# Attention, routed experts and a feed-forward block in one kernel: rows stored in token order, experts' rows found from summed lists

## The chip, the cores and the metric

The kernel runs on one core of one Trainium2 chip. The metric is the device time of one execution in microseconds (us). The kernel before took 825.89 us, the median of three runs (821.13 to 826.58).

## What is computed

Inputs are 4 batches of 8 heads, 768 positions and head size 48, so 3072 tokens of 384 numbers.

```python
# 1. attention with a decaying state, for each batch and head, t = 0..767
cur   = outer(u * k[t], v[t])
y[t]  = r[t] @ (state + cur)
state = w[:, None] * state + outer(k[t], v[t])
# 2. x = y as 3072 rows of 384; each row goes to one of 8 experts
logits     = (x / |x|) @ (emb / |emb|).T / tau
expert_idx = argmax(logits);  gate = softmax(logits)[expert_idx]
out[mask]  = gate * (relu(x[mask] @ w1[e]) @ w2[e])      # 384 -> 1024 -> 384
# 3. a dense block over all rows, 384 -> 2048 -> 384
h = out @ w_in;  result = (h * clip(h + 3, 0, 6) / 6) @ w_out
```

## The kernel before

**Attention.** Positions are cut into 6 chunks of 128 (`c`), heads into 4 pairs (`hp`): 24 groups in order `i = 4c + hp`. Each group (all four batches at once) runs on TensorE the scores `a_ps` (L642), the diagonal part `m_ps` (L654), the outputs `y_ps` (L665, L669), the state's update `u_ps` (L676) and the transposes `x_ps` (L690) that put the result into token rows `x_t`. ScalarE copies the scores out (`a_m`, L645) and GpSimd masks them (L646); VectorE makes the scaled operands (`k_s` L625, `r_s` L626), `mv` and `y_sb`. Loads for a group are issued four groups ahead on SyncE (SP).

**Routing.** When the four groups of chunk `c` are done, `route(c)` runs as a generator, one step a group, during chunk `c + 1`: logits, argmax and the one-hot `ohot`, then ranks by matmuls with a triangle and with ones. Before, the rank places a token inside its chunk with the tokens sorted by expert, and four indirect transfers a chunk (L274, GpSimd's queue) scatter the rows of `x_t` (384 numbers, the gate, padding) into `xs_d` in DRAM.

**The first expert early.** After three chunks (`c == KC and hp == 3`, i = 15), `leader` takes the expert with most tokens so far. `shift` and `lead_rows` compute from the chunks' counts where its rows lie, `x_rows` (L373) gathers 256 of them, and `x_cols` scales them by the gate (L384, ScalarE), transposes them on TensorE (L391) and splits them into a high and a low part `xh`, `xl` (L392, L393). When the attention ends, `expert(0, ...)` runs over these 256 columns, with the last chunk's routing, `late_rows` (where the leader's other rows lie), `order` (experts by size) and `all_rows` between its steps. Then a second pass with the same weights takes the next 256 rows of the leader, gathered only then (`late`, L870), and experts 1 to 7 follow with fixed widths of 444 down to 378 columns; the gather and the transposes for an expert run under the expert before it.

**An expert** is eight steps `f`: `l1(f + 2)` (nine matmuls into one bank), `l2(f)` (nine into three accumulators `acc`), then `between(f)`. Each product is three matmuls of float32r operands (high by high, low by high, high by low: L398 to L400), so a pass is 144 matmuls, each behind its own weight load of 128 columns.

**Order.** Within an engine, instructions keep the order that a planner gave them, which lays the program out by estimated times; matmuls marked `pin` keep program order, and `behind(x, n)` keeps `x` behind the instruction recorded under `n`. At run time each engine and each DMA queue takes its list strictly in order, so an instruction that waits holds up all behind it.

Of the kernel before, what the change touches and what calls it, by code (L numbers as in the profile page):

```python
# [8 lines left out]
F32 = mybir.dt.float32  # L9
# [25 lines left out]
NE = 256  # L35
NB = 512

CAPS = [NE, 444, 420, 408, 400, 392, 388, 378]
# [6 lines left out]
def rwkv_moe_kernel(ctx, tc, dT, tokA, wuT, uw, emb, tau, w1, w2, win, wout, out):  # L45
# [13 lines left out]
    y_d = dram.tile([NT, DM], F32, name="y_d")  # L59
    wf_d = [dram.tile([128, WCH], F32, name=f"wf_d{j}") for j in range(4)] if wide else None  # L60

    actx = ExitStack()
# [20 lines left out]
    wrk = st_p.tile([128, E * RPT * E], F32, name="wrk")  # L83
    zrow = st_p.tile([128, E * NT // 128], I32, name="zrow")
    nc.gpsimd.memset(zrow, 0)
    nums = const.tile([128, 3], F32, name="nums")
    three, hlf, viol = (nums[:, i:i + 1] for i in range(3))
# [9 lines left out]
    delta = const.tile([128, NCH, E], F32, name="delta")  # L97
# [20 lines left out]
    lead_i = const.tile([128, 2], I32, name="lead_i")  # L118
    n0 = lead_f[:, 1:2]
# [59 lines left out]
    def prep_w(j, lo_eng, after=None, st=None, later=None):  # L179
# [6 lines left out]
        def piece(c0):  # L186
            sl = slice(c0, c0 + WCH // 3)
            cp = nc.scalar.copy(out=hi[:, sl], in_=st[:, sl])
            if after:
                behind(cp, after)  # L190
# [3 lines left out]
            if after == "x_t":  # L194
                behind(sub, "y_s")
        for c0 in range(0, WCH, WCH // 3):
# [14 lines left out]
    def route(c, x_t, sm, xT, st_p, group="rows", pin=lambda i: i):  # L211
# [31 lines left out]
        aft = sm.tile([128, B, E], BF16, name="aft", tag="aft")  # L243
        nc.vector.tensor_tensor(out=aft, in0=iot, in1=idx_b, op=ALU.is_gt)
# [5 lines left out]
        rc_ps = psM.tile([128, B + 2, E], F32, name="r_ps", tag="m")  # L250
        r_ps, c_ps = rc_ps[:, 0:B], rc_ps[:, B:]
# [5 lines left out]
        for i, t in enumerate((oh, aft)):  # L257
            for b in range(B):
                pin(nc.tensor.matmul(c_ps[:, i], lhsT=ones, rhs=t[:, b], start=(b == 0), stop=(b == B - 1), skip_group_check=True))
        at = sm.tile([128, B, E], F32, name="at", tag="at")  # L260
        nc.vector.tensor_tensor(out=at, in0=r_ps, in1=oh, op=ALU.mult)
# [116 lines left out]
    def x_cols(rows, n, pool, width=NB, after=None):  # L378
# [3 lines left out]
        for t in range(rt):  # L382
            pn = min(128, n - t * 128)
            mul = nc.scalar.mul(rows[0:pn, t, 0:DM], rows[0:pn, t, 0:DM], rows[0:pn, t, DM:DM + 1])  # L384
            if after:
                behind(mul, after)
# [828 lines left out]
```

## Time and profile before

| | us |
|---|---|
| median of 3 runs | 825.89 |
| lowest, highest | 821.13, 826.58 |
| the profiled execution, its span | 824.2, 822.4 |

| engine | busy us | share of the span |
|---|---|---|
| PE (TensorE) | 784.0 | 95% |
| DVE (VectorE) | 494.7 | 60% |
| ACT (ScalarE) | 331.7 | 40% |
| POOL (GpSimd) | 218.9 | 27% |

The profile is one execution. PE's shares are highest from 205 us to the end, in the experts and the dense block. PEld is the weight load, which lies beside a matmul. A matmul's record is longer than the distance to the next one, since they are pipelined: the distance of starts is what one costs in a stream. "[3.40 <-ACT a_m L645]" behind an instruction means that its engine sat idle for 3.40 us before it and which instruction ended that.

### The profile page before, as it was taken

Reading aid. Unit: us, or ns where it says so; the run is one execution under the profiler, and the core shown is the slowest. Engines: PE = TensorE matmul, PEld = TensorE weight load, DVE = VectorE, ACT = ScalarE, POOL = GpSimd, SP = SyncE. Lnnn points to the kernel's source line nnn. Section 1 sums busy time; section 2 is a strip of 40 time slices with the busy share of each in tenths; the row PEclk is TensorE's granted clock in tenths of the full one; section 3 lists DMA queues with packets and bytes.
Section 4 is the critical chain, followed back from the end, with each engine's and each line's share of the span. In section 5 each row is a group of like instructions: output and inputs, shape, how many; then the busy total and the mean of one; then the engine's idle time right before and its main releaser. Section 6 shows DMA issues by size and latency. Waiting matters only on the chain. (4 is left out here: it accounts for less than half of the span.)

```text
span 822.4 us, 13576 instructions
## 1 busy us (share of the span) xinstructions
PE 784.0 (95%) x5178; PEld 698.3 (85%) x5179; DVE 494.7 (60%) x1014; ACT 331.7 (40%) x644; POOL 218.9 (27%) x239
## 2 busy tenths in 40 slices
PE   6899879889999999999999999999999999999994
PEld 4678666679999999998989998899999999999984
DVE  8789866463868777859478788552343334333331
ACT  3434435425455445545444333432333333333331
POOL 5667666443242144212101111210011002001001
PEclk9999998999999999999999999999999999999998
DMA  9968693234655566452322222110000001001001
GB/s 257 277 216 237 203 290 123 79 97 149 224 186 177 199 197 216 147 181 83 113 68 70 57 58 59 39 38 1 1 10 29 1 1 39 1 1 39 0 1 38
DMA packets 30552, 86.42 MB, mean 105 GB/s; under 512 B 4620, under 2 KB 12865, under 8 KB 30480
## 3 DMA queue, kind: packets, MB, share of 16 engines
q1 hardware_dynamic: 25312, 70.81, 28.2%
q0 software_dynamic: 5168, 14.68, 5.0%
q8 instruction: 42, 0.69, 0.4%
q14 instruction: 30, 0.25, 0.1%
HBM read 72.84 MB, written 12.63 MB: 104 GB/s over the span
## 5 line engine op out<-in xcount | busy, mean ns | idle before, releaser
L399 PE MATMUL l<-xl,whi 128*128 128x512 f32 (+8 forms) x504 | 186.4, 370 | 0.0
L398 PE MATMUL l<-xh,whi 128*128 128x512 f32 (+8 forms) x504 | 184.4, 371 | 1.9 <-DVEq L1074 1.6
L400 PE MATMUL l<-xh,wlo 128*128 128x512 f32 (+8 forms) x504 | 185.4, 369 | 0.0
L434 DVE SCALAR_TENSOR_TENSOR rg<-rg,l 128x512 f32<-128x512 f32 x96 | 65.8, 687 | 132.0 <-ACT rg L433 131.8
L433 ACT ACTIVATE rg<-l,nums 128x512 f32<-128x512 f32 x96 | 65.7, 689 | 169.8 <-PE l L400 160.1
L449 PE MATMUL o<-wlo,hh 128*128 128x384 f32 x384 | 128.6, 335 | 0.4 <-POOL wlo L1102 0.4
L448 PE MATMUL o<-whi,hh 128*128 128x384 f32 x384 | 128.0, 336 | 0.5 <-ACT hh L435 0.5
L450 PE MATMUL o<-whi,hl 128*128 128x384 f32 x384 | 123.9, 335 | 0.0
L398 PEld LDWEIGHTS l<-xh,whi 128*128 128x128 f32 x504 | 94.9, 189 | 13.4 <-issue 2.8
L400 PEld LDWEIGHTS l<-xh,wlo 128*128 128x128 f32 x504 | 95.1, 189 | 12.9
L399 PEld LDWEIGHTS l<-xl,whi 128*128 128x128 f32 x504 | 95.0, 189 | 10.2
L436 DVE TENSOR_TENSOR hl<-rg,hh 128x512 fp32r<-128x512 f32 x96 | 66.7, 697 | 43.5 <-ACT hh L435 42.9
L1132 POOL DMA_INDIRECT out_dram<-o_t,ctok x20 | 20.6, 1032 | 254.4 <-ACT o_t L1130 250.9
L435 ACT CAST hh<-rg 128x512 fp32r<-128x512 f32 x96 | 59.4, 621 | 68.4 <-DVE rg L434 52.5
L448 PEld LDWEIGHTS o<-whi,hh 128*128 128x128 f32 x384 | 72.0, 188 | 5.2 <-ACT hh L435 0.8
L449 PEld LDWEIGHTS o<-wlo,hh 128*128 128x128 f32 x384 | 72.1, 188 | 4.2 <-POOL wlo L1102 0.7
L399 PE MATMUL acc<-hl,whi 128*128 128x256 f32 (+7 forms) x216 | 71.8, 334 | 0.2 <-DVE hl L495 0.2
L450 PEld LDWEIGHTS o<-whi,hl 128*128 128x128 f32 x384 | 71.7, 188 | 0.3
L400 PE MATMUL acc<-hh,wlo 128*128 128x256 f32 (+7 forms) x216 | 72.0, 334 | 0.0
L495 DVE SCALAR_TENSOR_TENSOR hl<-l,hh 128x256 fp32r<-128x256 f32 (+7 forms) x72 | 38.1, 542 | 53.9 <-ACT hh L494 53.7
L494 ACT ACTIVATE hh<-l 128x256 fp32r<-128x256 f32 (+7 forms) x72 | 33.5, 481 | 91.6 <-PE l L400 88.7
L398 PE MATMUL acc<-hh,whi 128*128 128x256 f32 (+7 forms) x216 | 65.2, 335 | 0.7 <-DVE x L920 0.7
(215 smaller groups left out, 1176.0 us busy)
## 6 DMA issues: line engine op xcount, KB each, us to landing
wst<-in_w_dram SPq DMA_DIRECT2D x32, 768.0 KB, 4.3
rk_t<-in_dT_dram SPq DMA_DIRECT2D x24, 448.0 KB, 4.5
q<-in_win_dram SPq DMA_DIRECT2D x16, 384.0 KB, 3.3
q<-in_wout_dram SPq DMA_DIRECT2D x16, 384.0 KB, 3.3
vd<-in_dT_dram SPq DMA_DIRECT2D x24, 224.0 KB, 4.7
vt<-in_tok_dram SPq DMA_DIRECT2D x24, 224.0 KB, 4.5
tk<-in_tok_dram SPq DMA_DIRECT2D x24, 192.0 KB, 5.1
wf_d<-t SPq DMA_DIRECT2D x16, 192.0 KB, 4.1
```

The costliest lines, as they stand in the source:

```text
L398: pin(nc.tensor.matmul(ps, lhsT=w[0], rhs=x[0], start=first, stop=False))
L399: pin(nc.tensor.matmul(ps, lhsT=w[0], rhs=x[1], start=False, stop=False))
L400: pin(nc.tensor.matmul(ps, lhsT=w[1], rhs=x[0], start=False, stop=last))
L433: nc.scalar.activation(out=r6, in_=ps, func=AF.Relu, bias=three)
L434: nc.vector.scalar_tensor_tensor(out=gf, in0=r6, scalar=6.0, in1=ps, op0=ALU.min, op1=ALU.mult)
L435: nc.scalar.copy(out=gh, in_=gf)
L436: nc.vector.tensor_tensor(out=gl, in0=gf, in1=gh.bitcast(F32), op=ALU.subtract)
L448: pin(nc.tensor.matmul(acc[t], lhsT=gh[:, sl], rhs=wh[:, f % 4, :], start=(f == span[0]), stop=False))
L449: pin(nc.tensor.matmul(acc[t], lhsT=gh[:, sl], rhs=wl[:, f % 4, :], start=False, stop=False))
L450: pin(nc.tensor.matmul(acc[t], lhsT=gl[:, sl], rhs=wh[:, f % 4, :], start=False, stop=(f == span[1] - 1)))
L494: last["a"] = nc.scalar.activation(out=hh[:, 0:n], in_=ps[:, 0:n], func=AF.Relu).ins
L495: last["v"] = nc.vector.scalar_tensor_tensor(out=hl[:, 0:n], in0=ps[:, 0:n], scalar=0.0, in1=hh[:, 0:n].bitcast(F32), op0=ALU.max, op1=ALU ...
```

## The change

- Each chunk's rows go to `xs_d` in token order, one plain transfer a chunk on SP (`write`); the 24 scatters on GpSimd are gone.
- The rank now counts from the first chunk on (`cum` is added). VectorE makes two one-hots of each token, its row within a list's block of 128 (`at_row`) and its expert and block (`at_et`), and multiplies the second by the token's two digits (`who_et`). Four matmuls a chunk sum the digits at the token's place; `lists` adds the chunks up. A list entry is a row's number in `xs_d`. `shift`, `steps`, `late_rows`, `delta` and the matmuls over `aft` go.
- The early pass has 192 columns instead of 256, the late pass 256 as before, at a fixed place. The late rows are gathered during the early pass into a buffer of the attention (three transfers of 128 rows), and transposed before its last step.
- The early rows' scaling and transposes are spread over groups 18 to 21, each held behind that group's copies (`"x_t"`), and pinned on TensorE.
- The last chunk's third routing step moves behind `l1(2)`, and a fourth behind `l1(3)`; `order` and `all_rows` move two steps back, behind the list.
- The rare paths (`again`, `overflow`) and the places of conversion buffers follow; neither path runs here.

The core of the diff:

```diff
-NE = 256
+NE = 192
+NL = 256
...
-CAPS = [NE, 444, 420, 408, 400, 392, 388, 378]
+CAPS = [NE + NL, 444, 420, 408, 400, 392, 388, 378]
...
+    lp = ctx.enter_context(tc.tile_pool(name="lp", bufs=1))
...
+    nc.gpsimd.iota(row_i[:, 0:128], pattern=[[1, 128]], base=0, channel_multiplier=0)
...
+    nc.vector.tensor_copy(vals[:, :, 0], posn[:, 0:1].to_broadcast([128, NTILE]))
+    nc.vector.tensor_copy(vals[:, :, 1], row_i[:, 131:131 + NTILE])
...
-        for b in range(B):
-            pin(nc.tensor.matmul(r_ps, lhsT=ones, rhs=aft[:, b:b + 1, :].to_broadcast([128, B, E]), start=False, stop=False, skip_group_check=True))
...
-        dsti = sm.tile([128, B], I32, name="dsti", tag="dsti")
-        nc.vector.tensor_scalar(out=dsti, in0=rnk, scalar1=float(c * B * C), scalar2=None, op0=ALU.add)
...
-        nc.vector.tensor_tensor(out=delta[:, c], in0=c_ps[:, 1], in1=cum[:, c], op=ALU.subtract)
-
-        def scatter(b):
-            sc = nc.gpsimd.indirect_dma_start(out=xs_d[:, :], out_offset=bass.IndirectOffsetOnAxis(ap=dsti[:, b:b + 1], axis=0),
-                                              in_=x_t[:, b, :], in_offset=None, bounds_check=NT - 1, oob_is_err=False)
...
-        yield [lambda b=b: scatter(b) for b in range(B)]
+        if lists_too:
...
+            nc.vector.tensor_tensor(out=ge, in0=rnk.unsqueeze(2).to_broadcast([128, B, RPT - 1]), in1=row_f[:, 128:131].unsqueeze(1).to_broadcast([128, B, RPT - 1]), op=ALU.is_ge)
+            nc.vector.tensor_reduce(out=hi, in_=ge, axis=AX.X, op=ALU.add)
+            nc.vector.scalar_tensor_tensor(out=lo, in0=hi, scalar=-128.0, in1=rnk, op0=ALU.mult, op1=ALU.add)
+            nc.vector.scalar_tensor_tensor(out=et, in0=idx, scalar=float(RPT), in1=hi, op0=ALU.mult, op1=ALU.add)
...
+            nc.vector.tensor_tensor(out=at_row, in0=row_b.unsqueeze(1).to_broadcast([128, B, 128]), in1=lo.unsqueeze(2).to_broadcast([128, B, 128]), op=ALU.is_equal)
...
+            nc.vector.tensor_tensor(out=at_et, in0=row_b[:, 0:ET_].unsqueeze(1).to_broadcast([128, B, ET_]), in1=et.unsqueeze(2).to_broadcast([128, B, ET_]), op=ALU.is_equal)
...
+            nc.vector.tensor_tensor(out=who_et, in0=at_et.unsqueeze(2).to_broadcast([128, B, 2, ET_]), in1=vals[:, j0:j0 + B].unsqueeze(3).to_broadcast([128, B, 2, ET_]), op=ALU.mult)
+
+        def write():
+            loads["write"] = nc.sync.dma_start(out=xs_d.rearrange("(c b p) d -> c p b d", b=B, p=C)[c], in_=x_t).ins
+        yield [write]
+        l_ps = psM.tile([128, 2, ET_], F32, name="li_ps", tag="m")
+        for b in range(B):
+            pin(nc.tensor.matmul(l_ps, lhsT=at_row[:, b], rhs=who_et[:, b], start=(b == 0), stop=(b == B - 1)))
+        if c == 0:
+            nc.vector.tensor_copy(lists, l_ps)
+        else:
+            nc.vector.tensor_tensor(out=lists, in0=l_ps, in1=lists, op=ALU.add)
+        yield []
...
+    def lead_rows():
+
+        w = wrk[:, 0:2 * RPT * E].rearrange("p (v t e) -> p v t e", v=2, t=RPT)
+        sh = [128, 2, RPT, E]
+        nc.vector.tensor_tensor(out=w, in0=lists.rearrange("p v (e t) -> p v t e", e=E), in1=lead.unsqueeze(1).unsqueeze(1).to_broadcast(sh), op=ALU.mult)
...
         nc.vector.tensor_reduce(out=r, in_=w, axis=AX.X, op=ALU.add)
...
+        loads["list"] = nc.vector.scalar_tensor_tensor(out=ix0, in0=r[:, 1], scalar=128.0, in1=r[:, 0], op0=ALU.mult, op1=ALU.add).ins
...
+    LATE = [(t, 128) for t in range(NE // 128, RPT)]
...
+        parts = [scale] + [lambda k=k: third(k) for k in range(KD)]
...
+            mid(f)
             if f >= 0:
                 l2(f)
             between(f)
...
             if c == KC and hp == 3:
-                for f in rest:
-                    f()
-                rest = []
                 leader(cum[:, KC])
-
-                rows0 = x_rows(NE, e0p, ix0, KC * B * C)
+                rows0 = x_rows(in_rows(NE), e0p, ix0, tiles=2, known=KC * B * C)
...
-            if i == 20:
-                x0 = x_cols(rows0, NE, e0p, NE)
+            if i == 18:
+                x0 = x_cols(rows0, in_rows(NE), lp, NL, "x_t", cols, pin)
+            if cols and i >= 18:
+                cols.pop(0)()
...
+        def mid(f):
+            if f == 0:
+                for g in step(last_r, 1):
+                    g()
+            elif f == 1:
+                step(last_r, 1)
+                lead_rows()
+                late.append(x_rows(LATE, xp, ix0, "x", 2))
+                loads["late"] = loads["rows"]
 
         def between(f):
             if f == -2:
                 step(last_r, 1)
-            elif f == -1:
-                for g in step(last_r, 1):
+            elif f == 1:
+                chunks[3] = prep_w(3, nc.vector, "list", st3)
+            elif f == 2:
+                order("list")
+                all_rows()
+            elif f == NF1 - 2:
+                late.append(x_cols(late[0], LATE, lp, NL, later=cols, pin=pin, skip=NE % 128))
+                for g in cols[0:3]:
                     g()
-                late_rows()
-            elif f == 0:
-                order()
-                all_rows()
-            elif f == 1:
-                chunks[3] = prep_w(3, nc.vector, "relu", st3)
-        acc, _ = expert(0, x0, NE, between, pin)
+            elif f == NF1 - 1:
+                cols[3]()
+        late = []
+        acc, _ = expert(0, x0, NE, between, pin, mid)
...
-        late = x_rows(NE, mp, ix0[:, 2:4])
-        loads["late"] = loads["rows"]
...
-                dst = x2[d][:, bass.ds(at, n)]
+                dst = x2[d][:, bass.ds(at, n) if e else slice(NE, NE + NL)]
```

## Rows read from the trace of the kernel before

**Rows 1.** windows by chunk: busy us (instructions) PE, PEld, DVE, ACT, POOL; clock, DMA, GB/s

```profile
62.15:83.97 21.82, 21.82 (x312) 16.95 (x308) 20.15 (x45) 9.29 (x23) 17.45 (x19) 1.00 0.81 241
83.97:108.29 24.32, 22.20 (x312) 16.79 (x308) 21.67 (x64) 9.18 (x23) 17.10 (x19) 1.00 0.76 221
108.29:139.82 31.53, 27.30 (x313) 20.97 (x309) 19.11 (x46) 12.32 (x29) 19.98 (x23) 0.84 0.67 205
139.82:162.14 22.32, 18.79 (x219) 13.56 (x215) 11.88 (x35) 10.38 (x27) 10.80 (x11) 0.92 0.23 83
162.14:186.82 24.68, 19.62 (x172) 18.58 (x168) 13.44 (x62) 9.29 (x27) 8.79 (x10) 0.99 0.30 94
```

**Rows 2.** waits of PE over the span: us in total, times, longest

```profile
PE a_ps L642 <- ACT a_m L645: 3.4, 1, 3.4
PE tp L391 <- ACT rows L384: 3.4, 2, 2.6
...
PE tp L391 <- DVE xl L393: 1.8, 1, 1.8
...
PE r_ps L252 <- DVE ohot L242: 1.3, 1, 1.3
PE x_ps L690 <- DVE lead_f L312: 1.1, 1, 1.1
```

**Rows 3.** timelines of POOL and ACT around the early gather: start, us, instruction, wait before it

```profile
111.05 1.10 POOL L373 DMA_INDIRECT rows<-xs_d,ix  x1 [3.15 <-DMA xs_d<-x_t,dsti]
...
118.15 0.61 ACT L384 ACTIVATE rows<-rows 128x384 f32<-128x384 f32 x1 [7.33 <-DMA rows<-xs_d,ix]
```

**Rows 4.** timeline of PE, second and third group of chunk 4

```profile
120.84 2.56 PE L642 MATMUL a_ps<-r_s,k_s 48*128 48x128 f32 x16 [3.40 <-ACT a_m L645]
...
131.08 1.39 PE L642 MATMUL a_ps<-r_s,k_s 48*128 48x128 f32 x16
```

**Rows 5.** timelines of POOL, ACT and PE around the late rows

```profile
173.33 1.16 POOL L274 DMA_INDIRECT xs_d<-x_t,dsti  x1 [0.30 <-issue]
180.81 1.05 POOL L373 DMA_INDIRECT rows<-xs_d,ix  x1 [6.32 <-DVE hl L495]
...
184.12 0.61 ACT L384 ACTIVATE rows<-rows 128x384 f32<-128x384 f32 x1 [4.78 <-DMA rows<-xs_d,ix]
...
186.82 1.01 PE L398 MATMUL l<-xh,whi 128*128 128x256 f32 x3 [0.32 <-ACT xh L392]
...
191.74 0.61 PE L398 MATMUL acc<-hh,whi 128*128 128x256 f32 x3
```

**Rows 6.** DMA issues: KB each where known, median us from issue to landing

```profile
xs_d<-x_t,dsti POOLq DMA_INDIRECT x24, 4.2
```

**Rows 7.** groups by form, DVE: busy us, mean ns of one, idle before

```profile
L320 DVE TENSOR_TENSOR wrk<-place,prod 128x256 f32<-128x256 bf16 x1 | 0.6, 621 | 0.0
...
L353 DVE TENSOR_TENSOR prod<-place,iot 128x64 f32<-128x64 bf16 x1 | 0.2, 220 | 0.0
```

**Rows 8.** timelines of DVE and POOL, one operation of DVE with and without company

```profile
59.88 2.21 DVE L625 TENSOR_TENSOR k_s<-rk_t,itab 112x512 f32<-112x512 f32 x1
...
77.48 0.69 DVE L625 TENSOR_TENSOR k_s<-rk_t,itab 112x512 f32<-112x512 f32 x1
...
60.27 1.27 POOL L628 TENSOR_TENSOR rk_p<-rk_t 112x512 f32<-112x512 f32 x1
```

**Rows 9.** windows of PE alone: the pass of 256 columns, expert 1 at 444

```profile
168.00:180.00 12.00, 12.00 (x103) 1.00 0.40 134
216.00:228.00 12.00, 12.00 (x61) 1.00 0.59 197
```

**Rows 10.** groups by form: weight loads and plain f32 matmuls

```profile
L654 PE MATMUL m_ps<-rk_p,ub 112*112 112x512 f32 x48 | 28.6, 679 | 2.1 <-DVE mv L656 2.1
...
L642 PEld LDWEIGHTS a_ps<-r_s,k_s 48*128 48x128 f32 x384 | 25.5, 196 | 7.0 <-ACT a_m L645 3.7 <-issue 1.9 <-ACT ktab L580 0.2
...
L665 PEld LDWEIGHTS y_ps<-r_s,state 48*64 48x64 f32 x160 | 17.6, 137 | 5.9 <-issue 5.0
```

More of the change, by code (lines that the diff above doesn't have):

```diff
@@ L188, in piece @@
             cp = nc.scalar.copy(out=hi[:, sl], in_=st[:, sl])
-            if after:
+            if after and after != "list":
                 behind(cp, after)
@@ L195, in piece @@
                 behind(sub, "y_s")
+            if after == "list":
+                behind(sub, "list")
         for c0 in range(0, WCH, WCH // 3):
@@ L209, in inv_norm, with route @@
         return y
-    def route(c, x_t, sm, xT, st_p, group="rows", pin=lambda i: i):
+    def route(c, x_t, sm, xT, st_p, lists_too=False, pin=lambda i: i):
         j0 = c * B
@@ L269, in route @@
         nc.vector.reciprocal(out=x_t[:, :, DM:DM + 1], in_=gate.unsqueeze(2))
-        nc.vector.tensor_tensor(out=cum[:, c + 1], in0=c_ps[:, 0], in1=cum[:, c], op=ALU.add)
-        nc.vector.tensor_tensor(out=delta[:, c], in0=c_ps[:, 1], in1=cum[:, c], op=ALU.subtract)
-        def scatter(b):
-            sc = nc.gpsimd.indirect_dma_start(out=xs_d[:, :], out_offset=bass.IndirectOffsetOnAxis(ap=dsti[:, b:b + 1], axis=0),
-                                              in_=x_t[:, b, :], in_offset=None, bounds_check=NT - 1, oob_is_err=False)
-            tc.declare_no_dep(sc.ins, group=group, reason="each token has its own row of its chunk")
-            tc.add_to_no_dep_group(group, sc.ins)
@@ L376, in x_rows, with x_cols, scale, third @@
         return rows
[L378 to L379 removed]
+    def x_cols(rows, where, pool, width=NB, after=None, later=None, pin=lambda i: i, skip=0):
+        n = min(width, sum(w[1] for w in where) - skip)
         xh = pool.tile([128, KD, width], F32R, name="xh", tag="xh")[:, :, 0:n]
         xl = pool.tile([128, KD, width], F32R, name="xl", tag="xl")[:, :, 0:n]
[L382 to L386, printed above, removed]
[L387 to L393 removed]
+        def scale():
+            for t, pn in where:
+                mul = nc.scalar.mul(rows[0:pn, t, 0:DM], rows[0:pn, t, 0:DM], rows[0:pn, t, DM:DM + 1])
+                if after:
+                    behind(mul, after)
+        def third(k):
+            tp = psM.tile([128, NB], F32, name="tp", tag="m")
+            for i, (t, pn) in enumerate(where):
+                pin(nc.tensor.transpose(tp[:, i * 128:i * 128 + pn], rows[0:pn, t, k * 128:(k + 1) * 128], ident[0:pn, 0:pn]))
+            src = tp[:, skip:skip + n]
+            cp = nc.scalar.copy(out=xh[:, k, :], in_=src)
+            sub = nc.vector.tensor_tensor(out=xl[:, k, :], in0=src, in1=xh[:, k, :].bitcast(F32), op=ALU.subtract)
+            if after == "x_t":
+                behind(cp, "x_t")
+                behind(sub, "y_s")
+            loads["cols"] = sub.ins
+        parts = [scale] + [lambda k=k: third(k) for k in range(KD)]
+        if later is None:
+            for f in parts:
+                f()
+        else:
+            later.extend(parts)
         return xh, xl
@@ L692, in by_token @@
                            in_=x_ps.rearrange("p b (h d) -> p b h d", d=64)[:, :, :, 0:48]).ins
-        pend, rest, pieces = None, [], []
+        pend, rest, pieces, cols = None, [], [], []
         AHEAD = 4
```

208 lines of the change are left out of this document (101 added, 107 removed).

## The prediction

> **What bounds the kernel now.** I read the windows by chunk first, then the waits of PE, then the timelines around its two longest waits. PE is busy for 95% of the span, and its matmuls of experts 1 to 7 and of the dense block stay as they are; what can be won or lost lies before them. A chunk of attention that runs undisturbed takes 21.82 us, and PE is busy in all of it [rows 1]. The next one takes 24.32, the one after 31.53, at a mean granted clock of 0.84, and the last chunk up to the first matmul of the experts 22.32 at 0.92. From there to the second pass of the first expert there are 24.68 us.
>
> The waits say where this went: once 3.4 us for ScalarE's copy of the scores, 3.4 in two pieces for the late rows, 1.8 for the split of early rows, 1.3 and 1.1 for VectorE [rows 2]. The timelines tell why. ScalarE sat 7.33 us in front of the early rows' scaling, until their gather had landed at 118.15; the scores' copy stood behind it, though it had nothing to do with it. The gather itself had waited 3.15 us on GpSimd for the scatters to land [rows 3]. After its 3.4 us PE came back at the lower clock: the group that starts at 120.84 runs to 131.08, 10.24 us, where a quarter of the undisturbed chunk is 5.46 [rows 1, 4]. The late rows show the same chain: the fourth scatter starts at 173.33, the first gather at 180.81, its rows reach ScalarE at 184.12, and the second pass starts at 186.82; its first 27 matmuls take until 191.74 [rows 5].
>
> **The change part by part.** The sum is made against the profiled execution, 824.2 us (span 822.4); the median of the three runs is 1.7 higher.
>
> *Chunk 4 (108.29 to 139.82).* The scaling of the early rows is now held behind the copies of group 18, three groups after the gather is issued, so ScalarE no longer stands there in groups 16 and 17, and the four scatters that the gather waited for are one transfer on SP. If both work, the chunk falls back to an undisturbed one: 31.53 - 21.82 = 9.7 us less, the lower clock with it. What is late next is VectorE (below), so I book -9.0.
>
> *The write.* Its landing is not in the trace; the nearest row is the scatter's 4.2 us [rows 6]. It waits on SP for the gate, and the loads behind it wait too, but these run four groups (some 20 us) ahead of use, so a stop of a few us costs nothing; were that lead used up, each us would reach PE whole. GpSimd loses 24 scatters, some 1.2 us each [rows 5]; in undisturbed chunks PE waits for nothing there, so alone this is worth nothing.
>
> *VectorE.* Each chunk's lists add eight operations. Four are tiny, at most 0.22 us; the one-hot of 128 elements lies between 0.22 and 0.62; the product of 256 elements is taken at 0.62, its sum at 0.22 [rows 7]. The one-hot of 512 elements lies between 0.69 (512 in plain order, alone [rows 8]) and 1.16 (0.62 and the slope from 64 to 256 elements [rows 7] carried on). One more addition joins the rank; `aft`, `dsti` and `delta` go. Starts overlap a little, so I take 2 us net, bounds 1 and 3. In the undisturbed chunk VectorE was busy for 20.15 of 21.82 us [rows 1]: 22.15 is 0.3 over it, and bursts come on top. I book +0.7 for chunks 2 and 3, +0.8 for the rest; bounds 0 and 5 in all. In chunk 3 `leader` gets shorter by about what the list adds, so its 24.32 stays.
>
> An operation of VectorE next to GpSimd's product took 2.21 us where the same one alone took 0.69 [rows 8]. The Trainium skill, SBUF — State Buffer, "Who interferes with whom", states that a VectorE instruction with two SBUF inputs and a GpSimd instruction that reads SBUF lock each other out of a shared port pair. The trace agrees with it, and most of the added operations have two SBUF inputs: by that rule they wait for GpSimd, against this change (second rival).
>
> *Chunk 5.* The early rows' transposes come one third a group, so the wait of 1.8 goes, and the lower clock behind it: at a mean of 0.92, 16% of 22.32 us ran at 1.2 GHz, 3.6 us that need 1.8 at 2.4 GHz. -3.6; the number of transposes stays. I book -3.5.
>
> *The early pass.* 64 fewer columns in 144 matmuls. At 256 columns a matmul costs 12.00/103 = 116.5 ns, at 444 columns 197 ns: in proportion to the columns, 192 would cost 87 ns and the pass 4.2 us less [rows 9]. But each matmul has its own weight load. Loads of 128 and of 64 columns over 48 rows last 196 and 137 ns [rows 10]: 0.92 ns a column, 118 ns for 128 if one load follows another. That is already the 116.5 at 256 columns, so below it nothing falls. I take 0, the row being one of the same array and operand size; bounds 0 and -4.2.
>
> The Trainium skill, TensorE: Matmul & The Clock Gate, "LDWEIGHTS (loading the stationary operand)", gives the load as its columns over 1.2 per ns, 107 ns here; by it the pass would save 144 x 9.5 ns = 1.4 us. No run here shows a stream below 256 columns.
>
> *Late rows.* Let T be 162.14, the pass's first matmul. The write can be issued about where the first scatter was: three steps of some 1.5 us before 173.33 [rows 5], T + 6.7; it lands 4.2 later, T + 10.9 [rows 6]. The list's index is ready by then (`l1(3)`, four small matmuls, four operations of VectorE). Three gathers of 1.05 + 0.30 us follow; the third starts at T + 13.6 and is with ScalarE 3.3 us later as before (180.81 to 184.12), T + 16.9, scaled at T + 17.5. PE gets to the first transpose after 135 matmuls x 116.5 ns = 15.7 us and the routing's stops. Before, the stretch of 24.68 us [rows 1] less the waits of 3.4 and 0.32 for late rows [rows 2, 5] and some 1.2 of transposes left 19.8 for the pass and its stops, 3.0 more than 144 x 116.5 ns = 16.8; the 1.3 for the one-hot [rows 2] mostly goes, since `l1(2)` now lies in front, and the list's matmuls bring about as much. So T + 18.7: the rows are there 1.2 us earlier. With nine more matmuls and nine transposes (some 0.1 us each) the second pass starts at T + 20.9 instead of T + 24.7: -3.8. It no longer starts at the lower clock: 27 matmuls cost 3.1 us, not 4.9, less 0.2 for transposes in between: -1.6. If the narrower pass does run faster, the late rows bind at T + 17.5 and most of that gain is a wait.
>
> *Setup.* Three index rows on GpSimd and four conversions on VectorE, 1 us at most, ahead of waits for the first loads: 0, bound +0.5. Fixed place of the late columns: 0.
>
> Sum: -9.0 - 3.5 + 1.5 - 3.8 - 1.6 = -16.4, so 807.8 for the profiled execution, 809.5 by the median: **809**.
>
> **The rivals.**
> - *VectorE becomes the bound of the attention.* If three added operations a chunk lose 0.7 us to GpSimd, its chunk needs 20.15 + 2 + 2.1 = 24.3 us instead of 21.8, in four chunks +10 where 1.5 is booked: 817. For it: 20.15 of 21.82 busy, and 2.21 against 0.69 [rows 1, 8]. Against: GpSimd loses the scatters' 5 us a chunk and can make its products when VectorE is idle.
> - *The change doesn't do what it says in chunk 4.* The write waits on SP, or the planner puts the gather in front of the masks on GpSimd, and PE stands there again: 3.4 us plus 10.24 - 5.46 at the lower clock is 8.2 back, 818. For it: each queue is strictly in order, and the DMA share in this chunk is 0.67 on average. Against: the gather has three groups' time, and it took 7.
> - *The narrow pass falls to the rate of plain f32* (slower). No float32r matmul under 256 columns is in the trace, and the f32 ones cost much more: 28.6 us for 24 products of 512 columns, 1.19 us each, 0.45 us for 192 [rows 10]. Then 144 x (0.45 - 0.117) = 48 us are added: 857. It decides from 230 ns a matmul on, where it eats the 16.4. Against: from 444 to 256 columns the cost falls evenly.
>
> **How the numbers follow.** Forecast 0.60, VectorE 0.15, chunk 4 unmended 0.10, narrow pass slow 0.10, others 0.05, both ways. Within 1% is 817.6 to 834.2, about what a measurement of this kernel can't tell from no change. The forecast counts as faster, the second and third case lie on the edge (half each), so faster 0.72, same 0.17, slower 0.11. Range: down to 802 (lists free, pass partly in proportion), up to 821 (both middle cases with 3 us more); the narrow pass's case stays out.
>
> **What would show it.** Right: chunk 4 under 24 us at clock 1.00 and no wait of ScalarE for `rows` there; the second pass within 22 us of the first; 192 columns at 110 to 118 ns; VectorE over 95% in chunks 2 to 4. Wrong: waits of PE for `y_sb` or `r_s` in every chunk, a wait for the list's one-hots in the early pass over 1.5 us, transposes that wait for the late rows, or matmuls of 192 columns at 230 ns and more.

## The result and the profile after

The changed kernel takes 810.02 us (median of four executions, 809.04 to 812.18) where the kernel before, beside it, takes 824.07: a ratio of 0.9841, 95% interval 0.9808 to 0.9875. The profiled execution took 809.04 us, its span 807.4, against 824.2 and 822.4 before. Forecast was 809, faster. Repeated later beside other kernels, the change came out at 0.9869 (0.9821 to 0.9916), one disturbed execution left out. The time is right, in part by luck: the sum behind it is right in its largest term and wrong in several small ones that cancel.

Windows by chunk, changed kernel (busy us of PE, PEld, DVE, ACT, POOL, then granted clock, DMA share, GB/s); they answer to [rows 1]:

```profile
41.34:63.87 22.53, 22.07 (x309) 16.97 (x306) 19.70 (x52) 9.29 (x23) 12.69 (x15) 1.00 0.88 247
63.87:86.38 22.51, 22.05 (x309) 16.89 (x305) 19.67 (x49) 9.29 (x23) 12.65 (x15) 1.00 0.81 237
86.38:109.39 23.01, 22.09 (x309) 16.88 (x305) 20.91 (x59) 9.28 (x23) 14.13 (x15) 1.00 0.83 248
109.39:132.83 23.44, 22.25 (x311) 17.09 (x307) 21.49 (x51) 12.73 (x30) 13.73 (x15) 1.00 0.82 237
132.83:153.84 21.01, 18.30 (x212) 13.55 (x208) 14.67 (x41) 11.45 (x29) 7.78 (x9) 0.92 0.25 87
153.84:175.43 21.59, 18.52 (x171) 17.83 (x167) 13.40 (x60) 7.63 (x24) 5.90 (x8) 1.00 0.38 118
```

The stretch that took 31.53 us at a clock of 0.84 takes 23.44 at 1.00. The undisturbed ones have grown by 0.6 to 0.7 us, and the last chunk still shows 0.92. Waits of PE from 30 to 180 us (total, times, longest), against [rows 2]:

```profile
PE li_ps L302 <- DVE who_et L295: 4.9, 6, 1.2
PE r_ps L265 <- DVE ohot L257: 1.0, 1, 1.0
PE x_ps L711 <- ACT whi L201: 0.9, 1, 0.9
PE x_ps L711 <- DVE y_sb L699: 0.9, 1, 0.9
PE l_ps L243 <- ACT lt L236: 0.8, 1, 0.8
...
```

The waits for `rows`, `a_m` and `xl` are gone. One new wait stands in every chunk: the list's matmuls ask for one-hots that VectorE hasn't finished. The late rows (timelines of SP's queue, GpSimd, ScalarE and PE), against [rows 5]:

```profile
160.45 0.38 SPq L298 DMA_DIRECT2D xs_d<-x_t  x1
164.85 1.28 POOL L377 DMA_INDIRECT rows<-xs_d,ix  x1 [7.39 <-DVE ix L321]
171.53 0.62 ACT L389 ACTIVATE rows<-rows 128x384 f32<-128x384 f32 x1 [1.38 <-DMA rows<-xs_d,ix]
```

With T = 153.84 the write is issued at T + 6.6, the gather at T + 11.0, the last tile is scaled by T + 18.3, and PE takes it up at 173.79 without a wait. The 192-column matmuls, against [rows 9]:

```profile
164.43 0.27 PE L414 MATMUL l<-xh,whi 128*128 128x192 f32 x1
164.54 0.27 PE L415 MATMUL l<-xl,whi 128*128 128x192 f32 x1
164.65 0.27 PE L416 MATMUL l<-xh,wlo 128*128 128x192 f32 x1
```

Nine of them take 1.00 us, 111.3 ns each, where 256 columns took 116.5.

From the starts of the same matmuls in both traces, the 15.0 us of the span fall as follows (chunk 1 is 21.92 us before, chunk 4 is 31.53; `o` is the dense block's second product):

| part | forecast | measured |
|---|---|---|
| up to the first y_ps of chunk 1 (setup) | 0 | +1.1 |
| chunks 1 and 2 | part of +1.5 | +0.6, +0.7 |
| chunk 3 (leader) | 0 | -1.3 |
| chunk 4 | -9.0 | -8.1 |
| chunk 5, up to T | -3.5 | -1.3 |
| T to the second pass | -3.8 | -3.1 |
| lower clock in the second pass | -1.6 | -1.2 |
| second pass to the first `o` | 0 | +1.3 |
| first `o` to the last store | 0 | -1.95 |
| last store to the end | 0 | -1.9 |

The +1.3 is an accident of this pair of profiles and not a cost of the change. At the end of the experts TensorE stands twice in both, for 0.71 and 0.92 us before and for 0.56 and 0.92 in the changed kernel. The granted clock behind these waits stayed at 1.00 before and was lower in the changed kernel (windows of PE, PEld, DVE, ACT, POOL as above; first before, then changed):

```profile
384.00:394.00 10.00, 8.82 (x69) 8.49 (x70) 7.46 (x15) 3.67 (x9) 0.00 (x0) 1.00 0.22 79
371.00:381.00 10.00, 8.49 (x59) 8.16 (x60) 6.81 (x14) 2.96 (x6) 1.02 (x1) 0.83 0.22 79
```

It fell there in e5, e9 and e10 too, which have the code of before in the experts, and it did not in e2, e3, e8, e11 and e12, which have the changed one.

### The profile page after: what moved, and what is told of

Same layout as the page of the kernel before. It is cut to its first block, busy times and chain, and to the rows that moved or that the text cites. A ratio compares the mean times of both kernels' runs of the same rounds, so it can differ in the third digit from the quotient of the medians.

```text
span 807.4 us, 13475 instructions
## 1 busy us (share of the span) xinstructions
PE 780.8 (97%) x5157; PEld 695.5 (86%) x5158; DVE 498.4 (62%) x1030; ACT 332.1 (41%) x645; POOL 195.0 (24%) x219
## 5 line engine op out<-in xcount | busy, mean ns | idle before, releaser
L415 PE MATMUL l<-xl,whi 128*128 128x512 f32 (+9 forms) x504 | 186.1, 370 | 0.0
L416 PE MATMUL l<-xh,wlo 128*128 128x512 f32 (+9 forms) x504 | 185.4, 368 | 0.0
L414 PE MATMUL l<-xh,whi 128*128 128x512 f32 (+9 forms) x504 | 183.8, 369 | 1.6 <-DVEq L1110 1.6
L414 PEld LDWEIGHTS l<-xh,whi 128*128 128x128 f32 x504 | 94.7, 189 | 12.6 <-issue 2.8
L415 PE MATMUL acc<-hl,whi 128*128 128x192 f32 (+8 forms) x216 | 72.3, 336 | 0.2 <-DVE hl L515 0.2
L416 PE MATMUL acc<-hh,wlo 128*128 128x192 f32 (+8 forms) x216 | 72.3, 336 | 0.0
L515 DVE SCALAR_TENSOR_TENSOR hl<-l,hh 128x192 fp32r<-128x192 f32 (+8 forms) x72 | 37.5, 534 | 51.3 <-ACT hh L514 51.2
L514 ACT ACTIVATE hh<-l 128x192 fp32r<-128x192 f32 (+8 forms) x72 | 32.9, 473 | 85.2 <-PE l L416 82.4
L414 PE MATMUL acc<-hh,whi 128*128 128x192 f32 (+8 forms) x216 | 65.2, 335 | 0.6 <-DVE x L949 0.6
```

The lines of the kernel that those rows point to most:

```text
L414: pin(nc.tensor.matmul(ps, lhsT=w[0], rhs=x[0], start=first, stop=False))
L415: pin(nc.tensor.matmul(ps, lhsT=w[0], rhs=x[1], start=False, stop=False))
L416: pin(nc.tensor.matmul(ps, lhsT=w[1], rhs=x[0], start=False, stop=last))
L515: last["v"] = nc.vector.scalar_tensor_tensor(out=hl[:, 0:n], in0=ps[:, 0:n], scalar=0.0, in1=hh[:, 0:n].bitcast(F32), op0=ALU.max, op1=ALU ...
```

## The experiments

Lengths in us, from the same matmuls in each run's profile. Where the expectations say "chunks 2 and 3" for the two undisturbed ones (22.5 us), these are columns 1 and 2 here; chunk 4 is column 4 in both.

| run | y_ps of chunk 1 | 1 | 2 | 3 | 4 | 5 | T to pass 2 | ratio to before, 95% |
|---|---|---|---|---|---|---|---|---|
| before | 40.23 | 21.92 | 21.82 | 24.32 | 31.53 | 22.32 | 24.68 | |
| changed | 41.34 | 22.53 | 22.51 | 23.01 | 23.44 | 21.01 | 21.59 | 0.9841 (0.9808-0.9875) |
| e13 changed again | 43.50 | 22.53 | 22.51 | 23.02 | 23.45 | 21.09 | 21.41 | 0.9869 (0.9821-0.9916) |
| e4 scale not held | 41.25 | 22.54 | 22.51 | 23.03 | 29.81 | 21.86 | 20.71 | 0.9905 (0.9869-0.9942) |
| e5 before + hold | 38.44 | 21.93 | 21.82 | 24.36 | 30.23 | 18.66 | 23.17 | 0.9941 (0.9911-0.9970) |
| e9 + gather behind ny | 39.95 | 21.93 | 21.82 | 24.58 | 28.38 | 18.65 | 22.94 | 0.9920 (0.9894-0.9947) |
| e10 + pad behind ny | 38.45 | 21.93 | 22.16 | 27.33 | 22.99 | 21.01 | 22.39 | 0.9880 (0.9843-0.9917) |
| e1 list behind outputs | 42.09 | 22.02 | 21.99 | 22.25 | 25.49 | 18.41 | 20.87 | 0.9793 (0.9762-0.9825) |
| e2 lists constant | 41.04 | 21.73 | 21.62 | 21.62 | 26.98 | 18.45 | 18.36 | 0.9767 (0.9731-0.9802) |
| e7 not at leader | 44.16 | 22.02 | 21.99 | 25.75 | 22.61 | 18.40 | 19.51 | 0.9761 (0.9725-0.9798) |
| e11 all lists later | 41.61 | 22.01 | 21.99 | 22.37 | 24.68 | 18.41 | 19.52 | 0.9798 (0.9751-0.9845) |
| e12 + tables later | 37.24 | 22.02 | 21.99 | 22.37 | 27.39 | 20.58 | 19.52 | 0.9763 (0.9715-0.9811) |
| e8 late rows undone | 41.61 | 22.54 | 22.51 | 27.20 | 23.25 | 21.15 | 21.52 | 0.9824 (0.9797-0.9850) |
| e3 pass of 128 | 41.87 | 22.54 | 22.51 | 25.77 | 23.09 | 19.44 | 31.43 | 1.0005 (0.9980-1.0030) |

### What mended chunk 4

Theory: the hold on ScalarE's scaling mended it. Rival: the faster gather did. First the change without the hold (e4):

```diff
-                if after:
+                if after and after != "x_t":
                     behind(mul, after)
```

> The changed kernel, with the scaling of the early rows no longer held behind the copies of group 18, so that it stands early in ScalarE's order again; write and lists as in the change. Theory A (the hold is what mended chunk 4): ScalarE stands before the scaling until the gather lands, the scores' copy waits behind it, PE falls to the lower clock: chunk 4 goes from 23.4 back to some 30 us, total about 816. Theory B (the faster gather mended it: issued at 106.4 instead of 111.1 us, with no scatter to wait for, it lands near 111 to 113): ScalarE stands for 2 to 4 us, PE for less than 1, total 809 to 811.

Then the kernel before with the hold alone (e5), `x_cols` as in the change but fed by the scattered rows:

```diff
-            if i == 20:
-                x0 = x_cols(rows0, NE, e0p, NE)
+            if i == 18:
+                x0 = x_cols(rows0, NE, e0p, NE, "x_t", cols, pin)
+            if cols and i >= 18:
+                cols.pop(0)()
```

> The kernel before, scatters and all, with one part of the change alone: the scaling of the early rows held behind the copies of group 18, and their transposes one third a group. Theory A (the hold mended chunk 4): chunk 4 falls from 31.5 to 23 or 24 us at a clock of 1.00, the last chunk loses its wait of 1.8 us; 824 to about 814, so most of what the change gained in the attention. Theory B (without the plain write the gather still lands too late): the rows land at 118 us as before, the scaling now stands three groups later, near 122, so nothing should stand; if the scatters on GpSimd were the cause, chunk 4 stays above 27 us and the total above 819.

Neither theory holds alone. Without the hold chunk 4 is 29.81, with the hold but with scatters 30.23; only both together give 23.44. ScalarE stood 4.89 us before `rows` in e4 and not at all in e5, yet chunk 4 took nearly the same time. What both share is VectorE. Its waits for `ny` from the start of chunk 3 to 126 us (total, times, longest), in the kernel before:

```profile
DVE ny L207 <- POOL ny L206: 6.6, 2, 5.1
```

in e4, the change without the hold:

```profile
DVE ny L222 <- POOL ny L221: 5.2, 1, 5.2
```

in e5, the kernel before with the hold:

```profile
DVE ny L207 <- POOL ny L206: 6.4, 2, 4.9
```

and in the changed kernel:

```profile
DVE ny L222 <- POOL ny L221: 0.2, 1, 0.2
```

`ny` is the routing's power on GpSimd. VectorE takes its instructions in order, so while it stands before `ny`, the next `k_s` and `mv` stand behind it. In e4 `ny` is late because ScalarE, which makes its sums of squares (`junk`), stands before the rows (timelines of ScalarE and GpSimd):

```profile
113.03 0.61 ACT L389 ACTIVATE rows<-rows 128x384 f32<-128x384 f32 x1 [4.89 <-DMA rows<-xs_d,ix]
117.40 1.04 POOL L221 TENSOR_TENSOR ny<-ss,nums 128x4 f32<-128x4 f32 x1 [5.00 <-ACT junk L238]
```

In e5 it is late because GpSimd stood 2.94 us before the gather and took 2.4 more to issue it, and `ny` stands behind it there. The wait is put down to `r_s`, but the last scatter landed only at 108.29:

```profile
109.10 1.09 POOL L373 DMA_INDIRECT rows<-xs_d,ix  x1 [2.94 <-DVE r_s L637]
...
113.98 1.05 POOL L206 TENSOR_TENSOR ny<-ss,nums 128x4 f32<-128x4 f32 x1
```

Two chains end at the same operation; each alone costs nearly the whole. To test the second, e9 issued the gather behind `ny`:

```diff
+            if held:
+                tc.add_manual_dep(loads["rows"], loads["ny"].name, in_order, reason="the norm comes first")
```

> The kernel before with its scatters, the hold and the thirds of the run before (31.5 us in chunk 4 became 30.2), and one thing more: the early rows' gather is issued on GpSimd behind the routing's power (ny) of the next chunk and not in front of it. Theory A (two chains held TensorE in chunk 4: ScalarE in front of the rows, and VectorE for 4.9 us in front of ny, which stood on GpSimd behind the gather that waits for the scatters; cutting one leaves the other): chunk 4 falls to 23 to 24 us at the full clock, total from 818.9 to about 812, nearly the changed kernel's, with no plain write and no list. Theory B (the scatters themselves, their traffic and GpSimd's 1.2 us for each, hold chunk 4): it stays above 28 us, total 817 and more.

Chunk 4 went to 28.38 only, total 817.41. The prediction of 23 to 24 failed. GpSimd's timeline says why:

```profile
110.92 0.11 POOL L728 MEMSET x_t<- 128x12 f32 x1 [3.05 <-DMA xs_d<-x_t,dsti]
113.71 1.04 POOL L206 TENSOR_TENSOR ny<-ss,nums 128x4 f32<-128x4 f32 x1
114.95 1.14 POOL L373 DMA_INDIRECT rows<-xs_d,ix  x1 [0.20 <-DVE ny L207]
```

The gather no longer stands in front, but the clearing of the next buffer's pad columns does, and it waits for the same scatters. In e10 that too goes behind `ny`:

```diff
-                    nc.gpsimd.memset(xs[c][:, :, DM + 1:DG], 0.0)
+                    pad = nc.gpsimd.memset(xs[c][:, :, DM + 1:DG], 0.0)
+                    if i == 16:
+                        behind(pad, "ny")
```

> The kernel before with its scatters, the hold, the thirds and the gather behind ny as in the run before; in addition the clearing of the next x_t's pad columns on GpSimd stands behind ny. In the run before, GpSimd stood 3.05 us in front of that clearing until the scatters from the same buffer had landed, so ny came no earlier than when it stood behind the gather (113.7 us), VectorE waited 2.8 us for it and chunk 4 took 28.4. Theory A (it is the landing of the scatters, at whichever instruction GpSimd meets it first, that reaches TensorE through ny and VectorE): nothing in front of ny now waits for a scatter, VectorE no longer waits there, chunk 4 falls to 23 to 24.5 us at the full clock, total about 811 to 813. Theory B (the scatters cost by themselves): chunk 4 stays at 28, total 817.

```profile
112.48 1.04 POOL L206 TENSOR_TENSOR ny<-ss,nums 128x4 f32<-128x4 f32 x1 [1.23 <-ACT junk L223]
113.72 1.14 POOL L373 DMA_INDIRECT rows<-xs_d,ix  x1 [0.20 <-DVE ny L207]
116.18 0.12 POOL L728 MEMSET x_t<- 128x12 f32 x1
```

Chunk 4 took 22.99 us at the full clock, all 24 scatters still there; the median was 812.43 (808.47 to 820.56). So, once ScalarE's scaling is held back, chunk 4 is held by the order in which GpSimd meets the scatters' landing, not by the scatters' own time. The same clearing, which I had left in front in the other chunks, shows it once more: in e10's chunk 3 it waited 1.74 us, VectorE then 3.4 for `ny`, the clock fell, and the chunk took 27.33. So chunk 4 alone flatters e10: chunks 3 and 4 together took 55.85 us before, 52.96 in e9, 50.32 in e10 and 46.45 in the changed kernel. The 24.32 of chunk 3 before has a wait of 1.5 us of that kind; I had put it down to `leader`. TensorE's own waits there were 1.00 us for `ohot`, which follows `ny`, and 1.12 for leader's `lead_f`; in the changed kernel 0.20 for `a_m` and 0.72 for the list are left.

### What the lists cost

e1 puts the list's matmuls behind the outputs of their group:

```diff
-            if pend:
+            if pend and hp < HP - 1:
                 rest += step(pend, 1) or []
...
             ys[i] = outputs(c, hp, data[i][3], r_s, a_sbs.pop(i), kk, mvs.pop(i))
+            if pend and hp == HP - 1:
+                step(pend, 1)
```

> The changed kernel, with the list's four matmuls of a chunk put behind the outputs of their group instead of in front of them. Theory A (the list is only late: VectorE has its one-hots ready some 0.5 to 1.2 us after TensorE asks for them): the five waits of PE for who_et in the loop (0.46, 0.46, 0.72, 1.20, 0.87 us, 3.7 in all) go and nothing takes their place; chunks 2 and 3 go from 22.5 to about 21.9 us, and the last chunk also keeps the full clock (21.01 to about 19.3). From 809.0 to about 804.5 us for the profiled run. Theory B (VectorE is full in this stretch, and the wait only shows at the first place where TensorE asks): the same time turns up at y_sb, mv or r_s, the chunks stay at 22.5, total 808 to 810.

Chunks 1 and 2 fall to 22.02 and 21.99, chunk 5 to 18.41 at the full clock: theory A there. But chunk 4 grows to 25.49, since the leader's list, and with it gather and `ny`, come later. Median 806.86, not 804.5. e2 leaves the list work out:

```diff
...
-        if lists_too:
+        if False:
...
-        for b in range(B):
-            pin(nc.tensor.matmul(l_ps, lhsT=at_row[:, b], rhs=who_et[:, b], start=(b == 0), stop=(b == B - 1)))
```

> The changed kernel, with the lists written once at the start and neither the eight VectorE operations nor the four matmuls of the list in any chunk. Other rows are gathered than the reference wants, as many and as large. It prices the list work as a whole. Theory A (the list costs what the two undisturbed chunks show, 22.5 against 21.9 us before, and more at the end): chunks 2 and 3 at 21.8 to 21.9, the last one at about 19.5 with the full clock, the stretch up to the second pass 1.5 us shorter; 809.0 to about 803. Theory B (the 0.6 us a chunk come from something else, such as the write's traffic or the later start): within 1 us of 809.

803.67 us, chunks 1 to 3 at 21.6 to 21.7. So a chunk's list costs 0.8 to 1.4 us there; chunk 4 (26.98) is no measure of it, as there VectorE stood 7.2 us before writing the constant index, an accident of this kernel. e7 keeps the leader's list in front and moves the early pass's routing steps behind `l2`:

```diff
-            if pend and hp < HP - 1:
+            if pend and (hp < HP - 1 or c == KC):
...
-            if pend and hp == HP - 1:
+            if pend and hp == HP - 1 and c != KC:
...
```

> The changed kernel, with the list's matmuls behind the outputs as in the first run, but not in the group whose list the leading expert waits for (there it delayed the gather, and behind it ny, and chunk 4 grew from 23.4 to 25.5 us); in the early pass the three steps of the routing stand behind l2 of their step and not in front. Theory A (the waits were for a list that is late by no more than one group's outputs or one l2): chunks 2 and 3 at 22.0, chunk 4 at about 22.4, the last at 18.4 with the full clock, the stretch up to the second pass 1 to 2 us shorter (the rows are then ready just in time): 809 to about 803. Theory B (chunk 4 grows for another reason): chunk 4 at 25 us again, total 806 to 807.

Chunk 4 is 22.61 and T to the second pass 19.51, as theory A says, but the leader's chunk went from 23.01 to 25.75, and the total is 806.98, not 803. Its code there is the changed kernel's; e8 and e3 show the same. The timelines around the product for `who_et`, VectorE and GpSimd, in the changed kernel:

```profile
102.71 0.42 DVE L295 TENSOR_TENSOR who_et<-at_et,vals 128x256 bf16<-128x256 bf16 x1
101.97 2.26 POOL L667 TENSOR_SCALAR_AFFINE_SELECT a_m<-a_m 128x512 f32<-128x512 f32 x1
```

and in e8, with the PE instruction that waits:

```profile
103.14 1.48 DVE L295 TENSOR_TENSOR who_et<-at_et,vals 128x256 bf16<-128x256 bf16 x1
102.77 1.56 POOL L649 TENSOR_TENSOR rk_p<-rk_t 112x512 f32<-112x512 f32 x1
104.67 0.37 PE L302 MATMUL li_ps<-who_et,at_row 128*128 128x64 bf16 x4 [1.91 <-DVE who_et L295]
```

One time GpSimd's mask is the one that takes long (2.26 us; 46 of its 48 take 0.63 to 1.12), the other time VectorE's product beside GpSimd's. Then PE waits 1.91 us instead of 0.72 and comes back at the lower clock (mean 0.87 in that chunk). This is the rival "VectorE becomes the bound" in one chunk of some runs. e13 repeats the changed kernel:

> The changed kernel as it is, beside the last two on the same chip. In the profiles with its code up to the leader's chunk, the product for who_et took 0.42 us twice and 1.48 us three times (when it starts beside GpSimd's product of r and k), and TensorE then waited 0.72 or 1.8 to 1.9 us and lost 2.7 to 4.2 us more at the lower clock. Theory A (which of the two it is varies from run to run): the profile shows one of these two values again, and the times spread over 4 us or more, 808 to 813. Theory B (it is fixed by the code): 0.42 us again, 809 to 811.

0.42 us again, and every chunk as in the first profile to 0.1 us; its other executions lie between 809.20 and 815.04, and the profiled one differs from the first by 2.2 us at the start (43.50 against 41.34, at a mean granted clock of 0.80 against 0.83) and by nothing in the chunks. The spread is theory A's, the product theory B's. Whether it is the run or the program that decides between 0.42 and 1.48 stays open. e11 puts all lists behind the outputs and the gather behind `ny`, as e9 did:

> The changed kernel, with the list's matmuls behind the outputs in all five groups, the early pass's routing steps behind their l2, and the early rows' gather behind ny on GpSimd, so that a later list can't delay ny. Theory A (the list's price is a wait for one-hots that come late by less than a group's outputs): no wait of PE for who_et in the loop, chunks 22.0, 22.0, 22.3, 22.5, the last 18.4, the stretch up to the second pass 19.5; summed against 22.5, 22.5, 23.0, 23.4, 21.0, 21.6 that is 9 us, so 800 to 802. Theory B (one VectorE operation of 0.42 us that takes 1.48 beside GpSimd's product costs the same wherever the matmuls stand): a wait of 1 us and a lower clock appear at another tile in one of the chunks, total 804 to 807.

804.11 us, theory B's total. Chunks 1 to 3, 5 and the early pass are as theory A says, chunk 4 is 24.68 instead of 22.5, at the full clock: TensorE waits 0.56 us for `ohot` and 0.88 for `y_sb`, and the list's sum is now so late that the next chunk's `lt_ps` waits 0.8 us for it. e12 also builds the tables later:

```diff
...
+            if i == 3:
+                list_tables()
...
```

> The run before it, with the tables that the lists are made from (three index rows on GpSimd, four conversions on VectorE) built in the fourth group and not at the start. The first y_ps of chunk 1 came at 38.4 to 40.2 us in three kernels without these tables and at 41.0 to 44.2 in eight profiles with them. Theory A (the tables delay VectorE's powers, which the first products wait for): it comes at 39 to 40 us, total 1.5 us under the run before it. Theory B (the start differs from run to run, and the tables hide in front of the first loads): no difference outside of that scatter.

The first y_ps of chunk 1 comes at 37.24, and with 802.61 us (797.93 to 808.07) this kernel has the lowest median of all, 10 us under the changed one beside it; by the ratio to before, e7 and e2 are as fast. Over the profiles the start is 39.3 us without tables (four) and 42.1 with them (nine, e2 among them): they cost some 2.8 us, as theory A has it. How is less clear. VectorE's reciprocal of the first powers, which the first products wait for, starts at 5.74 us before, 7.26 in the changed kernel and 5.74 in e12. But the first `a_ps` then starts at 9.17, 9.46 and 8.93, only 0.3 to 0.5 us apart, and in e5, without tables, the reciprocal starts at 6.78 and the first y_ps of chunk 1 comes at 38.44 all the same. What differs by more is the clock. Windows up to that y_ps, before, in the changed kernel and in e12:

```profile
0.00:40.23 40.23, 31.93 (x289) 22.08 (x290) 32.75 (x59) 14.29 (x35) 24.73 (x52) 0.92 0.96 266
0.00:41.34 41.34, 35.80 (x289) 23.55 (x290) 30.98 (x63) 14.70 (x35) 24.32 (x55) 0.83 0.87 253
0.00:37.24 37.24, 31.91 (x288) 21.57 (x289) 32.45 (x63) 14.51 (x35) 26.96 (x55) 0.91 0.99 269
```

It is 0.91 or 0.92 in all five profiles without tables at the start and 0.80 to 0.84 in all nine with them, and TensorE needs about 4 us more for as many matmuls. That the tables bring the lower clock about is what e12 shows, which differs from e11 in them alone (41.61 against 37.24); by which wait they do it stays open.

e12's chunk 4 (27.39) and the lower clock that reaches from it into chunk 5 (20.58) lost again what the start gained; in chunk 4 two `wlo` took 4.03 us on VectorE beside GpSimd, 1.28 in the changed kernel, and `lt_ps` waited 2.6:

```profile
124.60 4.03 DVE L208 TENSOR_TENSOR wlo<-wst,whi 128x512 fp32r<-128x512 f32 x2
128.88 0.21 DVE L310 TENSOR_TENSOR lists<-li_ps,lists 128x64 f32<-128x64 f32 x1
129.14 1.93 PE L238 MATMUL lt_ps<-y_sb,enT 112*32 112x512 f32 x8 [2.58 <-DVE lists L310]
```

### The late rows

e8 gathers, scales and transposes them behind the early pass, as before:

```diff
-                late.append(x_rows(LATE, xp, ix0, "x", 2))
...
+        late.append(x_rows(LATE, mp, ix0))
+        xx = x_cols(late[0], LATE, lp, NL, skip=NE % 128)
...
```

> The changed kernel, with the late rows gathered, scaled and transposed behind the early pass, as before the change; write, lists and all else stay. Theory A (the late part is worth what the sum booked, 3.8 and 1.6 us, of which 4.3 showed): PE waits some 4 us for the rows behind the first pass and then runs at the lower clock; the second pass starts at T + 25 instead of T + 21.6 us, total 813 to 815. Theory B (the scatters were what made the late rows late, and the plain write has mended that already): the list is ready at T + 10.7 us, so a gather issued at once lands before the pass ends, wherever its line stands; within 1 us of 809.

Theory B: T to the second pass is 21.52, the total 809.68. The planner issues the gather as soon as the list is there, T + 11.4, wherever its line stands:

```profile
169.70 1.43 POOL L377 DMA_INDIRECT rows<-xs_d,ix  x1 [7.83 <-DVE ix L321]
176.13 0.62 ACT L389 ACTIVATE rows<-rows 128x384 f32<-128x384 f32 x1 [0.87 <-DMA rows<-xs_d,ix]
```

What made them late before was the wait for the scatters, not the place in the code. In the trace of before VectorE had written the index long since:

```profile
170.19 0.16 DVE L313 TENSOR_SCALAR ix<-lead_f 128x2 int32<-128x2 f32 x1
```

The fourth scatter, issued at 173.33, landed 6.5 us later, at 179.87, and the gather of [rows 5] started at 180.81; the operation of VectorE to which that row puts the wait is not the cause.

### The narrow pass

```diff
-NE = 192
+NE = 128
...
-CAPS = [NE + NL, 444, 420, 408, 400, 392, 388, 378]
+CAPS = [448, 444, 420, 408, 400, 392, 388, 378]
```

> The changed kernel, with the early pass 128 columns wide instead of 192 (the last 64 rows of the leading expert are left out of the result; the late pass keeps its 256 columns). It is read by the pitch of the 144 matmuls, 111.3 ns at 192 columns and 116.5 ns at 256 in the traces so far. Theory A (each matmul waits for its own weight load, whose length doesn't depend on the columns streamed): 110 to 112 ns again, total within 1 us of 809. Theory B (a part in proportion to the columns remains, by the 5 ns that the 64 columns from 256 to 192 gave): 105 to 107 ns, 0.8 us less. Theory C (in proportion, 58 ns): the pass is 7.7 us shorter, though the late rows, ready at T + 18.3, then hold back the second pass, so 1 to 2 us less in all.

The pitch is theory A's, 111.4 ns, as long as the clock is up. But the total was 824.58 us, which none of the three expected. Two matmuls before and two after the list's wait, from PE's timeline of that run:

```profile
158.72 0.28 PE L414 MATMUL l<-xh,whi 128*128 128x128 f32 x1
158.83 0.28 PE L415 MATMUL l<-xl,whi 128*128 128x128 f32 x1
...
170.74 0.41 PE L414 MATMUL l<-xh,whi 128*128 128x128 f32 x1
170.95 0.41 PE L415 MATMUL l<-xl,whi 128*128 128x128 f32 x1
```

and its windows over the pass and the start of the next:

```profile
160.00:165.00 5.00, 3.38 (x34) 3.19 (x34) 4.24 (x24) 0.84 (x4) 0.00 (x0) 0.80 0.44 159
165.00:170.00 5.00, 5.00 (x25) 5.00 (x25) 3.96 (x14) 0.74 (x2) 3.35 (x4) 0.50 0.29 79
175.00:180.00 5.00, 5.00 (x25) 5.00 (x25) 0.29 (x1) 0.34 (x2) 2.64 (x3) 0.50 0.94 344
186.65:192.00 5.35, 5.35 (x31) 5.22 (x31) 0.42 (x1) 1.00 (x4) 0.00 (x0) 0.65 0.00 0
```

After waits of 0.84 and 0.92 us, just ahead of the list's wait of 0.81, the clock fell to 0.50, 1.2 GHz, at 163.0, and stayed there for the rest of the 128-column pass; the pitch doubled to 212 ns. It rose only in the second pass, of 256 columns, at 190.3. The changed kernel's 192 columns, after waits of 0.80, 1.02 and 1.21 us, kept 1.00 throughout. 31.4 us instead of 21.6 for this stretch is the third rival in kind (a narrow pass that eats the gain), 64 columns further down, and by the clock, not by the rate of plain f32.

## Why the prediction was right, and where it was not

- **Chunk 4, -9.0 forecast, -8.1 measured.** The size is right and one cause was missed. I followed ScalarE's 7.33 us in front of the rows [rows 3] and took it for the chain; VectorE's 5.1 us before `ny` ended at nearly the same time and would have replaced it. e4 and e5 show it: each half of the change alone mends 1 to 2 us of 8. That the write, by taking the scatters away, also cuts the second chain was not in my working.
- **The write, 0.** It lands in 5.5 us (median of six, 3.6 to 9.6), not 4.2, and nothing on PE waits for it. GpSimd still meets its landing: the clearing of the next buffer stands 15.7 us in four waits for it. The write's worth is that GpSimd no longer stands in front of the gather: that is in chunk 4 and in the late rows.
- **VectorE's lists, +1.5.** Booked as busy time, they came as a wait: 4.9 us in six; chunks 1 and 2 grew by 0.6 and 0.7, of which 0.46 each is that wait. In chunk 5 wait and lower clock took back most of its term. The two-sided bound of 0 to 5 held; the value was low. The eight operations take 2.3 us a chunk (0.69 for the 512 elements, 0.42 for the product), as worked out; that VectorE's busy time still fell in chunk 2 (20.15 to 19.67) comes from its other operations: four `k_s` took 5.4 us in that chunk before and 3.2 now, four `r_s` 3.8 and 3.1. That the scatters' end freed them is likely, not shown. The sign "VectorE over 95% in chunks 2 to 4" failed: it is busy for 87 to 92%.
- **Chunk 5, -3.5.** e5, with the thirds and no list, shows 18.66: the term was -3.7. The changed kernel has 21.01: 0.95 us for `x_ps` behind ScalarE's `whi`, then 0.87 for the list, and the lower clock behind them. With the list behind the outputs (e1) it is 18.41; the wait for `whi` is still there, and the clock stays at 1.00.
- **Chunk 3, "stays 24.32".** Wrong by 1.3: TensorE's waits there went from 2.1 us to 0.9, see e10.
- **The early pass, 0.** The floor is nearly right: 111.3 ns, 0.8 us saved over 144 matmuls, not 4.2. Going down to 128 columns gave 111.4, so nothing of it is in proportion to the columns any more. That it is the weight load which sets it is not shown: in every run each load of the pass has 128 columns. The Trainium skill, TensorE: Matmul & The Clock Gate, "LDWEIGHTS (loading the stationary operand)", would give 107 ns; the runs have 4 ns more.
- **Late rows, -3.8 and -1.6.** -3.1 and -1.2. The steps came as forecast (write T + 6.6 for T + 6.7, rows T + 18.3 for T + 17.5); the pass with its stops took 19.95 us up to the transposes where I had 18.7, because TensorE waits three times, 0.80 us for `lt`, 1.02 for the one-hot and 1.21 for the list, where I had allowed for one wait of 1.3.
- **Setup, 0, bound +0.5.** The one term that lies outside its stated bound: +1.1 in this pair, some 2.8 over the profiles. I priced the tables by their own length, ahead of waits for the loads, and not by what a later start does to the clock: 0.83 where before had 0.92.
- **Not booked at all: 3.8 us gained.** First `o` to last store takes 399.5 or 401.1 us in the four profiles with scatters and 397.5 or 399.1 in the ten with the write; the higher of each two has a stretch at the lower clock. The 1.95 us lie at two waits of 0.5 and 0.4 us for `hh` and `wlo`, which are gone, and at the slower matmuls right behind them. The diff's new buffers for the dense weights' conversion touch that path, but I did not test them. Last store to end is 8.36 in the four and 6.40 to 6.48 in the ten. The store lands 2.6 us after its issue in both; what is shorter is GpSimd's closing DRAIN instruction, 7.73 us before and 5.86 now. Why, I don't know.
- **The rival "VectorE becomes the bound"** is seen in one chunk of three profiles out of the six with that code, for 2.7 to 4.2 us. The Trainium skill, SBUF — State Buffer, "Who interferes with whom", says that such a product, with two inputs in SBUF, and a GpSimd operation that reads SBUF exclude each other; 0.42 against 1.48 beside `rk_p` agrees.

So 809 was reached by -12.6 us up to the second pass and its first matmuls (forecast -16.4), +1.3 by an accident of the clock and -3.8 that I never named. That these add up to the forecast is luck.

## What to carry to other kernels

Where an engine stands for long, follow every engine that stands at the same time, not the one whose wait is longest: two chains that end together have to be cut together, and each cut alone looks worthless. An in-order queue that meets a transfer's landing passes the wait on to whatever stands behind it, and moving the first instruction only hands it to the next (gather, then clearing). A list or a table that is "a few short operations" is priced by who is next in line on its engine, and by the lower clock that can follow when TensorE waits.

## What was not expected of the hardware

- A stream of 128-column matmuls, one weight load each, ran at 1.2 GHz from 163 us to its end at 186 (e3); the 192 columns of the changed kernel ran at 2.4 GHz after waits as long.
- One VectorE product of 256 bf16 elements took 0.42 or 1.48 us, a pair of f32 subtractions 1.28 or 4.03, with GpSimd at work beside it; with TensorE's wait and lower clock behind it, the product moved a chunk by 2.7 to 4.2 us (e3, e7, e8).
- From the last store's issue to the end of the span: 8.4 us with the scatters in the program, 6.4 to 6.5 without; the whole difference is GpSimd's last DRAIN (7.73 us before, 5.86 in the changed kernel).
